# A mixer layer on one core: first column-mean by halves, start-up filler products gathered, and a new written-out order

## The chip, the core and the metric

The kernel runs on one core of a Trainium2 chip. The core has five instruction streams that the text names as the profile does: PE (matrix products), DVE (vector), ACT (activation), POOL (a second vector-like engine) and SP (which here issues the transfers). The metric is device time in microseconds (us); lower is better. All times are of the whole program.

## The reference, cut to what matters

Input is one sequence of 2048 rows of 512. With `xn = layernorm(x)`:

```python
qkv = xn @ wqkv                      # 32 heads of 16
logits = einsum(q, k at 8 positions, 2 apart, looking back) * 16**-0.5   # masked below 0
s = (softmax(logits) @ v) @ wo
y = layernorm(xn)
g = silu(gelu(y @ w1 + b1) @ w2 + b2)        # 512 -> 1376 -> 512
out = x + s * g
```

## The kernel before, in words

The 2048 rows are split by parity into two classes `c` (attention looks back in steps of 2, so each class is closed), and each class into eight tiles of 128 rows, numbered `i` 0 to 7. The heads are split into four blocks `hb`. A unit `u` is one class and one block: `qkv` makes its queries, keys and values on PE, `attention` does the eight-position softmax on DVE with help from POOL and ACT, and the MLP (`mlp1`, `mlp2`) fills PE between. Precise products are made from half-precision high and low parts, so that most products come in three passes: high by high, low by high, high by low.

All work of the opening concerns class 0. The names that matter:

- `xt[i]`, for the tiles 6 and 7 (`FP`): a copy of the tile that arrives already transposed, stored in `U`. `center(i)` subtracts each row's mean: for tile 6 the sum over the four column blocks is taken first (`f`) and one product with a constant matrix, `mean1`, spreads the mean; for tile 7 four products do all of it (L682). The subtraction itself is L693. `direct(i)` then makes the tile's q, k, v in full precision from the raw weights `stq[0]` (L700), tile 6 into `pl`, tile 7 into a bank named `z`.
- The other tiles are normalised row by row: statistics on DVE (L659, L660, L714, L716), a power on POOL (L718), the scaling on POOL, ACT or DVE (L748, L744, L751), the split into high and low parts `yT`, and the transposition: for the tiles 0 to 3 on PE (L766, then the split by L770 to L773), for the tiles 4 to 7 by a transfer of the split parts (L756 to L758).
- `scale_q(hb)`: the sum of squares of a block of weights (L597 on ACT, L513 on PE, L524 to L542 on DVE) gives its scale `qsc`; `prep_q(hb)` makes the high part `wq` on ACT (L619) and the low part (L626 on DVE, L553 and L554 on POOL). `wq_82` and `wq_83` in listings of the order are the blocks 0 and 1.
- `qkv` products are L864; the results leave their bank by L878 on DVE or L882 on ACT.
- Filler products (L1305): `WAKE` products of constants, whose result nobody reads. They are the only PE work that serves no output.

Transfers of the opening are issued by SP one after the other: `t` (the transposed tiles 6 and 7, 256 KB each), `q` (half a block of weights, 384 KB), `x` (a tile, 256 KB), `w` (weights of the MLP).

`Plan` records every operation with what it reads and writes. `Plan.issue` then places the operations in the order of the table `ORDER`, a list of operation numbers; each engine receives its own operations in that order and the waits between engines follow from the reads and writes. So the table alone decides what stands ahead of what on each engine, transfers included, and which buffer of a ring an operation gets.

## Time and profile before

| | us |
|---|---|
| median of three timed runs | 413.33 (413.1 to 413.67) |
| the profiled execution, its own time | 412.45 |
| its span, first to last instruction | 410.6 |
| PE busy | 403.6 |
| DVE busy | 381.7 |
| ACT busy | 225.3 |
| POOL busy | 132.8 |

The profiled execution is 0.9 us below the median of the timed runs. Its span leaves out 1.85 us around it. In a chain row, the columns are start, duration and what ran; in a timeline row start, duration, engine, line, operation and, in brackets, the idle time before it with its releaser. A row `x4` merges four records; a full-precision product leaves two records on PE.

### The profile page before, as it was taken

The page shows a single profiled execution, that of the slowest core. Times are in us where ns is not written, and L with a number is a line of the kernel's source. Part 1 is how long each engine was busy: PE and PEld are TensorE (multiplying, and loading weights), DVE is VectorE, ACT ScalarE, POOL GpSimd, SP SyncE. Part 2 cuts the span into 40 slices and gives each one's busy share as a digit, 9 for nine tenths or more (in the row PEclk, how much of TensorE's full clock was granted, in tenths as well). Part 3 has the DMA queues.
Part 4 walks back from the last instruction along what each step waited for, and adds up shares of the span by engine and source line. Part 5 has one row for each costly group of instructions (what it writes and reads, how often), then busy time and mean ns, then how long its engine had stood idle before and what let it go on. Part 6 is the DMA issues. An engine that isn't in the chain of part 4 may idle for free.

```text
span 410.6 us, 5500 instructions
## 1 busy us (share of the span) xinstructions
PE 403.6 (98%) x2035; PEld 199.3 (49%) x2035; DVE 381.7 (93%) x386; ACT 225.3 (55%) x372; POOL 132.8 (32%) x141
## 2 busy tenths in 40 slices
PE   7999999999999999999999999999999999999996
PEld 4665544444444455445544554444445544444443
DVE  4999999999999999999889999899999989989985
ACT  4899987983989736633564164114523177236310
POOL 3833000053552434243423344233322505250012
PEclk9999999999999999999999999999999999999999
DMA  8947437240018372911251008610244462004874
GB/s 300 388 105 233 165 110 199 89 180 26 1 30 197 77 130 79 165 32 27 51 145 23 0 2 215 208 51 25 104 120 122 107 137 59 0 1 117 271 209 180
DMA packets 52627, 48.04 MB, mean 117 GB/s; under 512 B 37066, under 2 KB 37510, under 8 KB 52088
## 3 DMA queue, kind: packets, MB, share of 16 engines
q1 hardware_dynamic: 52600, 47.69, 41.8%
q8 instruction: 16, 0.26, 0.3%
q14 instruction: 11, 0.09, 0.1%
HBM read 24.40 MB, written 7.34 MB: 77 GB/s over the span
## 4 chain that ended last, share of the span: by engine, by line
PE 97%; DVE 1%; DMA 1%; ACT 0%; issue 0%; ACTq 0%; DVEq 0%
PE ps L864 30%; PE ps L1143 25%; PE z L1186 25%; PE ps L1056 5%; PE z L1088 2%; PE ps L1088 2%; PE z L1174 2%; PE pl L864 1%; PE pl L700 1%; DMA U<-in_A_xt_dram 1%; PE pl L1088 1%; PE z L700 1%; PE z L1177 1%; PE z L766 1%; PE z L1305 0%; DVE U L1120 0%
## 5 line engine op out<-in xcount | busy, mean ns | idle before, releaser
L864 PE MATMUL ps<-wq,yT 128*128 128x384 f16 (+1 forms) x708 | 129.3, 337 | 0.1
L1186 PE MATMUL z<-w,h 128*128 128x512 f16 x480 | 111.4, 379 | 0.0
L1143 PE MATMUL ps<-yT,w 128*128 128x512 f16 x480 | 109.1, 379 | 0.0
L864 PEld LDWEIGHTS <-yT 128*128 128x128 f16 x744 | 72.3, 98 | 58.5 <-issue 1.1
L930 DVE TENSOR_TENSOR prod<-U 128x2048 f32<-128x2048 f32 x32 | 73.8, 2312 | 4.1 <-ACT U L882 3.0
L1143 PEld LDWEIGHTS <-w 128*128 128x128 f16 x480 | 46.7, 98 | 55.6 <-issue 0.5
L933 DVE TENSOR_REDUCE L<-prod 128x128 f32<-128x2048 f32 x32 | 73.0, 2282 | 0.5
L1186 PEld LDWEIGHTS <-h 128*128 128x128 f16 x480 | 46.5, 98 | 54.6 <-issue 0.7
L999 POOL TENSOR_TENSOR prod<-prod,prod 128x1024 f32<-128x1024 f32 x14 | 41.3, 2970 | 81.4 <-DVE prod L988 81.4
L882 ACT ACTIVATE U<-ps,cs 128x384 f32<-128x384 f32 x54 | 30.2, 577 | 62.9 <-PE ps L864 62.7
L988 DVE TENSOR_TENSOR prod<-pl,U 128x2048 f32<-128x2048 f32 x28 | 63.5, 2283 | 0.3
L1156 ACT ACTIVATE ps<-ps,b1T,hsc 128x512 f32<-128x512 f32 x40 | 29.9, 748 | 37.2 <-PE ps L1143 37.0
L1159 ACT ACTIVATE h<-ps,hsc 128x512 f16<-128x512 f32 x40 | 27.4, 685 | 20.5 <-PE z L1186 19.5
L1009 POOL COPY gate<-prod 1x1 f32<-1x1 f32 x21 | 4.6, 221 | 102.2 <-DVE prod L930 102.2
L1010 POOL TENSOR_TENSOR prod<-prod 128x1024 f32<-128x1024 f32 x14 | 32.8, 2346 | 0.0
L1161 DVE SCALAR_TENSOR_TENSOR h<-ps,hsc,h 128x512 f16<-128x512 f32 x40 | 29.5, 744 | 3.3 <-ACT h L1159 3.3
L1056 PE MATMUL ps<-wo,oT 128*128 128x512 f16 x96 | 21.5, 379 | 0.0
L983 DVE TENSOR_TENSOR prod<-prod,prod 128x2048 f32<-128x2048 f32 x9 | 20.6, 2288 | 0.2
L971 ACT ACTIVATE o<-prod,osc 128x1024 f16<-128x1024 f32 (+1 forms) x9 | 9.5, 1052 | 18.1 <-DVE prod L983 9.9
L1010 POOL TENSOR_TENSOR prod<-prod,prod 128x1024 f32<-128x1024 f32 x7 | 16.4, 2347 | 0.0
L1088 PEld LDWEIGHTS <-oT 128*128 128x128 f16 x108 | 10.5, 98 | 10.4 <-issue 0.2
L1056 PEld LDWEIGHTS <-oT 128*128 128x128 f16 x96 | 9.4, 98 | 11.1
(201 smaller groups left out, 397.2 us busy)
## 6 DMA issues: line engine op xcount, KB each, us to landing
f<-in_A_x_dram SPq DMA_DIRECT2D x31, 256.0 KB, 3.1
U<-U SPq DMA_DIRECT2D x16, 392.0 KB, 6.2
gd<-f SPq DMA_DIRECT2D x12, 256.0 KB, 4.3
prod<-in_A_x_dram SPq DMA_DIRECT2D x8, 256.0 KB, 6.2
oT<-in_B_w_dram SPq DMA_DIRECT2D x2, 1024.0 KB
yT<-in_B_w_dram SPq DMA_DIRECT2D x2, 1024.0 KB
f<-gd SPq DMA_DIRECT2D x8, 256.0 KB, 5.0
out_dram<-f SPq DMA_DIRECT2D x8, 256.0 KB
```

The lines of the kernel that those rows point to most:

```text
L864: nc.tensor.matmul(b.t[:, 0:wide], y[:, s, k, o:o + P], wq[hb][:, t, k], start=(n == 0), stop=(n == 11))
L882: act(384, lambda i=i, b=b: nc.scalar.activation(U3[:, i:i + 31:15, :], b.t[:, 0:384].rearrange("p (t e) -> p t e", t=3), AF.Identity, sca ...
L930: dve(2048, lambda p2=p2, g=g: nc.vector.tensor_tensor(p2(), q, slots(Ut, KH, 2 * g), op=ALU.mult), qk + [("kh", ub, 0), ("kh", ub, 1), (" ...
L933: dve(2048, lambda pr=pr, g=g: nc.vector.tensor_reduce(L3()[:, 2 * g:2 * g + 2], pr.t.rearrange("p (r f d) -> p r f d", r=2, d=DH), AX.X, ...
L988: dve(2048, lambda: nc.vector.tensor_tensor(pr.t.rearrange("p (r f d) -> p r f d", r=2, d=DH), A3()[:, 2 * g:2 * g + 2].rearrange("p r (f ...
L999: pool(2.4, lambda n=n: nc.gpsimd.tensor_tensor(acc.t[:, n:n + 1024], acc.t[:, n:n + 1024], p1.t[:, n:n + 1024], op=ALU.add), [acc, p1], [ ...
L1010: nc.gpsimd.tensor_tensor(x.t[:, 0:1024], x.t[:, 0:1024], y(), op=ALU.add)
L1056: nc.tensor.matmul(b.t, oT[:, hb, i // 4, s, i % 4], wo[:, t, hb], start=(hb == 0 and n == 0), stop=(hb == last and n == 2))
L1088: nc.tensor.matmul(b.t[:, cols], oT[:, hb, i // 4, s, i % 4], wo[:, t, hb, cols], start=(start and hb == 0 and n == 0), stop=(stop and hb ...
L1143: nc.tensor.matmul(b.t[0:M], w1[:, s, f * 512 + k * M:f * 512 + (k + 1) * M], yT[ch][:, t, k], start=(n == 0), stop=(n == 11))
L1156: act(512, lambda: nc.scalar.activation(b.t[0:M], b.t[0:M], AF.Gelu_apprx_tanh, bias=b1T[0:M, f:f + 1], scale=hsc[0:M, 1:2]), [b, ("b1T",) ...
L1186: nc.tensor.matmul(z.t, hl[s][:, t * P:(t + 1) * P], w2[:, w, f], start=(f == 0 and n == 0), stop=False)
```

## The change

Three things are edited.

The column sum of tile 6 was one reduction on DVE that reads the 512 columns in a strided view. It becomes two additions that are issued together: the two halves of 256 columns added, then the two 128-column halves of that. The reduction stays in the code, unused.

The number of filler products goes from 24 to 23, and the table places them differently: 19 in a row ahead of the mean product of tile 6 and four right behind it, none later. Before there were seven ahead, three behind, and fourteen singly or in small groups up to 56 us.

The table `ORDER` is another one. It has one number fewer, so that numbers above the filler products are shifted by one; taken with that shift, most operations stand within some twenty places of where they stood, throughout the program, and in the opening the transfers stand in another order. The lines of the kernel after are four higher from `center` on (L864 is L868).

```diff
-MEANBY = ('dve', 'pe', 'pool', 'pool')
+MEANBY = ('halves', 'pe', 'pool', 'pool')
 ...
 ORDER = (
-    0, 1, 240, 19, 2, 3, 4, 5, 6, 7, 8, 9, 10, 11, 133, 129, 113, 120, 112, 115, 130, 20, 21, 32, 33, 168, 114,
+    4, 0, 9, 1, 2, 32, 33, 239, 37, 38, 19, 39, 110, 111, 112, 113, 114, 115, 116, 117, 118, 119, 120, 121, 122,
 ...
-WAKE = 24
+WAKE = 23
 ...
         elif MEANBY[n] == "dve":
             dve(512, lambda: nc.vector.tensor_reduce(f3()[:, 0], x3.rearrange("p k t -> p t k"), AX.X, ALU.add),
                 [("xt", i)], [f], port=False, c=0.45)
+        elif MEANBY[n] == "halves":
+            with pl.fuse():
+                dve(256, lambda: nc.vector.tensor_tensor(f3(), x3[:, 0:2], x3[:, 2:4], op=ALU.add), [("xt", i)], [f])
+                dve(128, lambda: nc.vector.tensor_tensor(f3()[:, 0], f3()[:, 0], f3()[:, 1], op=ALU.add), [f], [f])
```

The transfers of the opening, in the order in which SP issues them (`x0` is tile 0, `q0` and `q2` are the two halves of weight block 0, `q4` and `q6` those of block 1):

| | |
|---|---|
| before | t6, q0, q2, x2, x0, q4, t7, x5, x1, x3, x4, q6, w0, w2, x7, w3, x6, w1, b1 |
| after | x0, t6, x3, q0, q2, x1, t7, x2, q4, x4, x5, w3, q6, x6, x7, w0, w2, w1, b1 |

## Prediction

> **What bounds the kernel now.** I read the page's busy line first:

> ```profile
> PE 403.6 (98%) x2035; PEld 199.3 (49%) x2035; DVE 381.7 (93%) x386; ACT 225.3 (55%) x372; POOL 132.8 (32%) x141
> ```

> Then busy time by stretches of the span (columns: stretch, its length, then busy time and instructions of PE, PEld, DVE, ACT, POOL, the granted clock, the DMA share, GB/s):

> ```profile
> 6.10:30.00 23.90, 23.84 (x132) 14.56 (x133) 20.88 (x60) 19.75 (x39) 13.70 (x12) 1.00 0.80 277
> 60.00:400.00 340.00, 339.91 (x1691) 163.47 (x1690) 323.90 (x271) 175.23 (x285) 110.30 (x114) 1.00 0.38 98
> ```

> From 6.1 to 30 us PE stands idle for 0.06 us, from 60 to 400 us for 0.09. So a gain has three sources only: PE's needed work starts earlier, PE does less that nobody needs, or it does the same faster. From 30 us on the new order can lose and, but for fillers, cannot win. The last additions and stores are the same operations on both sides. That leaves the opening, read in the chain of waits, in order of time (start, duration, what ran):

> ```profile
> 4.54 0.81 PE ps L691 x2
> 5.37 0.70 DVE U L693
> ...
> 6.11 2.93 PE pl L700 x4
> 9.04 0.21 PE z L1305
> ...
> 9.29 0.78 PE pl L700 x2
> 10.06 0.89 PE ps L682 x8
> 10.95 0.65 PE pl L700 x2
> 11.60 0.33 PE z L1305 x3
> ...
> 12.06 0.44 PE z L766 x4
> 12.50 2.58 PE z L700 x8
> 15.10 0.66 PE z L766 x4
> ...
> 17.52 0.64 PE z L766 x4
> 18.16 0.65 PE ps L864 x4
> ...
> 18.95 2.94 PE ps L864 x16
> ...
> 56.17 0.11 PE z L1305
> ```

> Three things are to be seen. The same eight passes over 384 columns take 2.58 us for tile 7 and 2.93 + 0.78 + 0.65 = 4.36 us for tile 6: the first four run at half pace. Then filler products (L1305) stand in the chain: fourteen in eleven rows from 9.04 to 56.17, 1.68 us together. Last, some rows are longer than their work, by waits too short to be named: a transposition (L766) takes 0.44, and twice 0.66 and 0.64; four L864 take 0.65, sixteen should take 2.60 and take 2.94.

> **The half pace.** The granted clock reads 1.00 in every stretch above, so only the durations show it. They change by 9.29 us, after PE had work from 4.54 on. Fillers of the start ran like this (start, duration):

> ```profile
> 1.19 1.65 PE L1305 MATMUL z<-first,fours 128*128 128x256 bf16 x7 [1.19 <-DVE first L440]
> ```

> That is at most 0.24 each, and PE then rested until 4.54. In the kernel after, 19 fillers at 0.21 to 0.24 fill 1.2 to 5.2 or 5.7 us, the mean product and four more follow, so that PE works from 1.2 to nearly 7, longer than the 4.7 us that it took before. I take the passes of tile 6, which now come after 9 us, at full pace.

> [...]

> **When the loads land.** A transfer's landing is seen where an engine started on it with nothing else to wait for:

> ```profile
> 3.46 1.02 DVE L685 TENSOR_REDUCE f<-U 128x128 f32<-128x512 f32 x1 [1.95 <-DMA U<-in_A_xt_dram]
> 4.50 0.84 ACT L597 ACTIVATE wq<-prod 128x768 bf16<-128x768 f32 x1 [2.49 <-DMA prod<-in_A_wqkv_dram]
> 6.35 0.69 DVE L659 BATCH_NORM_STATS2 bn<-prod 128x6 f32<-128x512 f32 x1 [0.29 <-DMA prod<-in_A_x_dram]
> 7.55 0.69 DVE L659 BATCH_NORM_STATS2 bn<-prod 128x6 f32<-128x512 f32 x1 [0.29 <-DMA prod<-in_A_x_dram]
> 8.50 0.84 ACT L597 ACTIVATE wq<-U 128x768 bf16<-128x768 f32 x1 [2.02 <-DMA U<-in_A_wqkv_dram]
> ```

> These are t6, q0, x2, x0 and q4, that is 256, 640, 1280, 1536 and 1920 KB into the stream; the last step is 384 KB in 0.95 us. With the same stream in the new sequence x0 lands at 3.46, t6 (512 KB) near 4.1, q2 (1536) at 7.55, x1 (1792) near 8.2, t7 (2048) at 8.50 + 128 x 0.95 / 384 = 8.82, x2 (2304) near 9.45.

> **The change part by part.** *Halves.* The rows price one addition of 256 columns; that of 128 lies below it.

> ```profile
> 404.56 0.41 DVE L1127 TENSOR_TENSOR U<-U 128x256 f32<-128x256 f32 x1
> ```

> The 128 columns lie between nothing and 0.41; I take 0.3, so 0.7 stands for 1.02 and 0.3 us is saved. It doesn't count: t6 is now the second load, DVE takes tile 0's statistics first, and the mean product moves from 4.54 to about 5.2. On PE nothing needs tile 6 before 9 us.

> *PE's opening.* Before, the first products of tile 6 stand ahead of the sums of weights (L513), and the mean of tile 7 (L682) behind three passes of them:

> ```order
> L700 MATMUL pl_146<-prod_100,U_94 128x384 x2
> L1305 LDWEIGHTS fours
> L1305 MATMUL z_147<-first,fours 128x256
> L513 LDWEIGHTS fours
> L513 MATMUL z_147<-s_126,fours 128x1
> L513 LDWEIGHTS fours
> L513 MATMUL z_147<-s_126,fours 128x1
> L700 MATMUL pl_146<-prod_100,U_94 128x384
> L682 MATMUL ps_144<-U_94,first 128x128 x4
> ```

> After, behind the last filler (L704 is L700 before, L770 is L766):

> ```order
> L1309 MATMUL z_147<-first,fours 128x256
> L513 LDWEIGHTS fours
> L513 MATMUL z_147<-s_125,fours 128x1
> L770 MATMUL z_150<-first,prod_100 128x128 x4
> L513 LDWEIGHTS fours
> L513 MATMUL z_147<-s_125,fours 128x1
> L682 MATMUL ps_144<-U_94,first 128x128 x4
> L704 MATMUL pl_146<-prod_101,U_94 128x384 x2
> L704 MATMUL z_148<-prod_101,U_94 128x384 x2
> ```

> So everything of weight stands behind L682, which waits for t7: PE's unbroken stretch starts at 8.82 instead of 6.11, plus 2.71. Ahead of it only the transposition of tile 0 is done, minus 0.44. The half pace falls into fillers: 4.36 - 2.58, minus 1.78. The fourteen late fillers go: minus 1.68. The short waits in the rows above (0.22 + 0.20 + 0.34) belong to the old order, minus 0.76; new ones take their place.

> *New wait one*: z_148 needs tile 7 centred. On DVE this stands behind the statistics of tile 1, the scale of the weights and the statistics of tile 2:

> ```profile
> 7.08 0.18 DVE L660 BATCH_NORM_AGGREGATE mv<-bn 128x2 f32<-128x6 f32 x1
> 9.36 0.16 DVE L524 TENSOR_SCALAR ssq<-z 128x1 f32<-128x1 f32 x1 [0.71 <-PE z L513]
> 9.87 0.69 DVE L659 BATCH_NORM_STATS2 bn<-prod 128x6 f32<-128x512 f32 x1
> ```

> Statistics take 0.91 (6.35 to 7.08, and 0.18), the scale 0.51 (9.36 to 9.87); its sums need q2, squared from 7.55 on by a pass of 0.84 and its read-out, so they are there near 8.9 and it doesn't wait. From x1 at 8.2 that makes 9.1, 9.6 and 10.5; a small operation of 0.1 and the subtraction of 0.70 follow: 11.3 to 11.4. PE stands there at 8.82 + 0.89 (mean) + 1.29 (two products for pl) = 11.0. Plus 0.4.

> *New wait two*: ACT. Before, both halves of block 1 are made late, between exits of finished banks:

> ```order
> L504 ACTIVATE wq_84,s_129<-h_113 128x4x96
> L756 CAST f_104<-prod_102 128x512
> L619 ACTIVATE wq_83<-U_94,qsc 128x768
> L882 ACTIVATE U_93<-ps_145,cs_118 128x3x128
> L619 ACTIVATE wq_83<-U_94,qsc 128x768
> L882 ACTIVATE U_93<-ps_143,cs_118 128x3x128
> ```

> After:

> ```order
> L504 ACTIVATE wq_84,s_129<-h_113 128x4x96
> L746 ACTIVATE rb_155<-pb_154,rb_155 128x1
> L748 ACTIVATE prod_102<-prod_102,rb_155 128x512
> L760 CAST f_104<-prod_102 128x512
> L619 ACTIVATE wq_83<-U_94,qsc 128x768
> L774 CAST yT_89<-z_147 128x4x128
> L619 ACTIVATE wq_83<-U_94,qsc 128x768
> L774 CAST yT_89<-z_150 128x4x128
> ```

> The exits and one large sum of squares move behind, and PE asks sooner: its first product with block 1 stands behind 12 products of block 0, before behind 36. ACT's work can be priced from start to start:

> ```profile
> 9.99 2.13 ACT L619 ACTIVATE wq<-prod,qsc 128x384 f16<-128x384 f32 x4 [0.56 <-DVE qsc L542]
> 18.18 0.28 ACT L742 ACTIVATE rb<-pb,rb 128x1 f32<-128x1 f32 x1
> 18.50 0.81 ACT L744 ACTIVATE prod<-prod,rb 128x512 f32<-128x512 f32 x1
> 19.22 0.51 ACT L504 ACTIVATE wq<-h 128x384 bf16<-128x384 f32 x1
> 19.73 0.60 ACT L756 CAST f<-prod 128x512 f16<-128x512 f32 x1
> 20.23 0.93 ACT L619 ACTIVATE wq<-U,qsc 128x768 f16<-128x768 f32 x1
> ```

> ACT starts 0.63 us behind L524 (9.36 to 9.99), so at 9.1 + 0.63, about 9.8. From there I leave it no rest: 2.1 (block 0), twice 1.05 (sums of squares of block 1: a pass of 0.84 and its read-out), twice 1.04 (scaling of tiles 1 and 4, 18.18 to 19.22), 0.51, 0.50 (a cast), 0.93, 0.5 (the cast L774), 0.93, together 9.6: it ends at 19.4. PE, from 11.4, has six direct products at 0.65 (3.9), three transpositions (1.32) and twelve L868 (1.95): 18.5. Plus 0.9.

> **The sum.** 2.71 - 0.44 - 1.78 - 1.68 - 0.76 + 0.4 + 0.9 = -0.65, rounded -0.7. Behind this point the products are as many as before, and I count nothing. On the profiled execution's 412.45 this is 411.8; its gap to the median of 413.33 is taken as that execution's, and the forecast is 413.33 - 0.7 = 412.6 us. What is sure of it: pace and fillers are rows. What isn't: t7's landing (8.5 to 9.2), the two new waits (each from nothing to 1.5), the old short waits (0 to 0.76). Without new waits and with t7 early it is -2.2, or 411.1. With both at their upper end and no old wait saved it is +1.8, or 415.1, which needs all three at once.

> **The rivals.** *ACT sets the pace (slower).* Place: the second high half of block 1 (L619). Each us that ACT rests between 9.8 and 19.4 is one on PE. The forecast turns into a loss of 0.8 when that L619 ends at 20.9 instead of 19.4. For: the scaling of tiles 1 and 4 waits for POOL's power, behind DVE's statistics, behind two loads. Against: the wait ahead of L619 in the row above is 0.56 us, none there is of 1.5. Price: 2 us of delay gives 413.33 + 1.3 = 414.6. Chance 0.11.

> *The pace falls back.* Between the last filler, near 6.8, and 8.82 PE has one transposition and two small sums. If this rest lowers the pace again, the mean of tile 7 takes 0.89 more and two products for pl 1.29 more, 2.2; the two new waits swallow 0.4 and 0.9 of it, and 0.9 is left: 413.5. For: before, the rest from 2.84 to 4.54 stood ahead of 4.7 us at half pace. Against: the pace had not risen when that rest came. Chance 0.1.

> [...] No row here shows a pace that falls.

> *The change doesn't do what it says: PE isn't the bound.* DVE is 93% busy, and its chain of attention could hold the end, so that PE's head start is given back in a wait later: 413.3; or PE, under the new table, meets a wait for DVE that the old one avoided, 414.6 if it is 2 us. For: the long stretch without a gap is the old table's merit, and the new one moves operations throughout. Against: DVE rests 16 us of 340 there, PE 0.09. Chance 0.24, 0.1 of it for the wait of 2 us.

> *More than forecast.* The new waits don't come, since ACT and DVE have the loads of x sooner: 411.1 to 412.4. Chance 0.25.

> **How the numbers follow.** The forecast has 0.3, its own range 412.0 to 413.1. About 0.2%, 0.83 us, is what a measurement can tell from no change; faster means under 412.5. Of the forecast half lies there, of "more than forecast" nearly all: 0.15 + 0.25 = 0.4. Slower by over 0.83 (over 414.16): the ACT rival's 0.11, the later wait's 0.1 and 0.03 of the others: 0.24. The rest, 0.36, is within. The range holds 8 of 10: from 411.2, leaving out a tenth at the low end, to 414.6.

> **What would show it.** Right: the first L704 passes at 0.33 each; L682 starting near 8.8 behind a load; no L1309 behind 7 us; PE idle before the first wq_83 product, released by ACT L619, 0.5 to 1 us; none from 30 to 405. Wrong: passes of 0.64 behind 9 us; a PE gap behind 60 us; L682 before 8.2 or behind 9.5; ACT's second L619 of wq_83 ending behind 20.5.

## The result and the profile after

The kernel after takes 414.97 us (median of 20 runs, 412.41 to 417.59) against 413.16 (412.48 to 413.86) for the kernel before: ratio 1.004, interval 1.003 to 1.0051. It is slower by 1.8 us where 0.7 less was forecast, and the median lies above the range of 411.2 to 414.6. The spread is a result by itself: before, it is 1.4 us, after, 5.2.

The profiled execution of the kernel after is one of its short ones: 412.92 us, span 411.1. Its PE stretches, in the columns of the prediction (the second is chosen from the mean of tile 7 to the first twelve products `pl`), and the waits of PE behind 10 us (in total, how often, the longest):

```profile
6.10:30.00 23.90, 21.00 (x118) 12.95 (x118) 20.74 (x58) 20.78 (x39) 11.50 (x11) 1.00 0.81 275
9.69:27.74 18.05, 17.84 (x98) 11.09 (x99) 17.32 (x52) 17.15 (x31) 10.21 (x10) 1.00 0.74 270
60.00:400.00 340.00, 339.45 (x1689) 163.14 (x1688) 323.35 (x270) 176.78 (x289) 110.22 (x109) 1.00 0.38 95
```

```profile
PE ps L868 <- ACT U L886: 0.5, 1, 0.5
PE ps L868 <- ACT wq L619: 0.2, 1, 0.2
```

PE starts its unbroken work later and then is as tight as before, with one new gap of 0.5 us between 60 and 400 us. The chain of waits of the kernel after begins so:

```profile
3.54 6.10 DMA U<-in_A_xt_dram
9.64 0.04 issue
9.69 1.16 PE ps L682 x8
10.85 1.29 PE pl L704 x4
12.14 1.54 PE z L704 x4
...
18.48 0.58 ACT yT L774
19.06 0.84 ACT wq L619
19.90 0.04 issue
19.95 7.96 PE ps L868 x48
```

The load of tile 7 leads, as forecast, but ends at 9.64, not 8.82. From there all is at full pace: four passes take 1.29 or 1.54 us, where the first four took 2.93 before. At 19.95 the wait for ACT's block 1 has come as named, worth 0.21 us. On PE ahead of that (timeline):

```profile
1.19 3.81 PE L1309 MATMUL z<-first,fours 128*128 128x256 bf16 x19 [1.19 <-DVE first L440]
5.16 0.49 PE L695 MATMUL ps<-f,first 128*128 128x128 f32 x2 [0.17 <-DVE pb L720]
5.49 0.60 PE L1309 MATMUL z<-first,fours 128*128 128x256 bf16 x4
7.38 0.16 PE L513 MATMUL z<-s,fours 128*128 128x1 bf16 x1 [1.29 <-ACT wq L597]
7.48 0.63 PE L770 MATMUL z<-first,prod 128*128 128x128 f32 x4
9.34 0.16 PE L513 MATMUL z<-s,fours 128*128 128x1 bf16 x1 [1.23 <-ACT wq L597]
```

Between 6.1 and 9.7 us PE rests, in two waits for ACT's squares, which wait for the loads of q0 and q2. Here nothing came of it. In most other executions something did. The 20 timed runs fall into three groups by the mean granted clock of the run, which leaves out the half pace ahead of the first rise (the profile of before has a mean of 1.000 with its four passes of 2.93 us at 6.11):

| mean granted clock | runs | time, us (median) |
|---|---|---|
| 0.999 to 1.0 | 3 | 412.41 to 412.92 (412.71) |
| 0.995 to 0.996 | 7 | 413.84 to 414.83 (414.17) |
| 0.991 to 0.992 | 10 | 415.1 to 417.59 (415.4) |

In the kernel before every run of the later comparisons has 0.998 to 1.0. Half a clock through 3.41 us, the step between the changes in e0's profile, lowers the mean over a span of some 412 by 0.5 x 3.41 / 412 = 0.0041, so the groups fit none, one and two stretches of 3.41 us at half pace; the profile of e0, with one, has a mean of 0.995, that of h1, with two, 0.992. A mean of 0.998 is no such stretch: at the very end of the program, where PE has no work left, the clock falls once more (in the profile of after it is 1.00 from 407.2 to 410.6 us and 0.54 from there to 411.1; the last product ends at 407.18). In e6's profile, with a mean of 0.998, the 0.002 make 1.6 us at half, worked out from its span of 411.7. The next section shows the stretches.

### The profile page after: what moved, and what is told of

The parts are those of the page before. It is cut to its first block, busy times and chain, and to the rows that moved or that the text cites. A ratio compares the mean times of both kernels' runs of the same rounds, so it can differ in the third digit from the quotient of the medians.

```text
span 411.1 us, 5501 instructions
## 1 busy us (share of the span) xinstructions
PE 402.3 (98%) x2034; PEld 199.0 (48%) x2034; DVE 381.5 (93%) x387; ACT 225.8 (55%) x373; POOL 132.4 (32%) x141
## 4 chain that ended last, share of the span: by engine, by line
PE 92%; DVE 3%; DMA 1%; issue 1%; ACT 1%; SPq 1%; DVEq 0%
PE ps L868 27%; PE ps L1147 25%; PE z L1190 24%; PE ps L1060 5%; PE z L1092 2%; PE ps L1092 2%; PE z L1178 2%; DMA U<-in_A_xt_dram 1%; PE pl L868 1%; PE z L704 1%; PE pl L704 1%; PE pl L1092 1%; PE z L1181 1%; DVE lw L643 1%; DVE L L937 1%
## 5 line engine op out<-in xcount | busy, mean ns | idle before, releaser
L868 PE MATMUL ps<-wq,yT 128*128 128x384 f16 (+1 forms) x708 | 128.1, 337 | 0.8 <-ACT U L886 0.5
L868 PEld LDWEIGHTS <-yT 128*128 128x128 f16 x744 | 72.5, 98 | 59.2 <-issue 2.3
L886 ACT ACTIVATE U<-ps,cs 128x384 f32<-128x384 f32 x54 | 30.5, 578 | 78.5 <-PE ps L868 61.9
L1003 POOL TENSOR_TENSOR prod<-prod,prod 128x1024 f32<-128x1024 f32 x14 | 37.3, 2683 | 98.6 <-DVE prod L992 71.7
L1014 POOL TENSOR_TENSOR prod<-prod,prod 128x1024 f32<-128x1024 f32 x7 | 16.4, 2346 | 0.0
L1092 PEld LDWEIGHTS <-oT 128*128 128x128 f16 x108 | 10.5, 98 | 10.4 <-DMA oT<-o 0.2
```

The lines of the kernel that those rows point to most:

```text
L868: nc.tensor.matmul(b.t[:, 0:wide], y[:, s, k, o:o + P], wq[hb][:, t, k], start=(n == 0), stop=(n == 11))
L886: act(384, lambda i=i, b=b: nc.scalar.activation(U3[:, i:i + 31:15, :], b.t[:, 0:384].rearrange("p (t e) -> p t e", t=3), AF.Identity, sca ...
L1003: pool(2.4, lambda n=n: nc.gpsimd.tensor_tensor(acc.t[:, n:n + 1024], acc.t[:, n:n + 1024], p1.t[:, n:n + 1024], op=ALU.add), [acc, p1], [ ...
L1014: nc.gpsimd.tensor_tensor(x.t[:, 0:1024], x.t[:, 0:1024], y(), op=ALU.add)
L1092: nc.tensor.matmul(b.t[:, cols], oT[:, hb, i // 4, s, i % 4], wo[:, t, hb, cols], start=(start and hb == 0 and n == 0), stop=(stop and hb ...
```

## The experiments

Two theories stood beside each other. **P**: the pace falls back in PE's rest. **L**: the loads of the opening land later and at times that change from run to run.

**e0: the kernel after, once more.**

> The kernel after, once more, as the control of this group. Theory P (the pace falls back: PE rests from about 6.1 to 9.7 us but for 0.9 us of work, and in most executions this takes the array to half pace for one or two stretches of 3.4 us): times in clusters near 412.5, 414.2 and 415.4 us, with mean granted clocks of 1.000, 0.996 and 0.992, and a profile of one of the slower ones shows passes of 0.64 us somewhere between 7 and 17 us. Theory L (the spread comes from loads that land at different times): times spread without clusters, and the clock does not follow them.

414.61 us (412.99 to 416.02), ratio 1.0035 (1.002 to 1.005); clocks 0.992 to 0.996 in all 12 runs. So the falls are there, but the times don't cluster as P expected: the nine runs with one stretch lie between 412.99 and 415.39, the three with two between 414.84 and 416.02. Something else spreads them too. The profile shows a fall. PE by stretches of 3.41 us, cut at the changes of the granted clock (stretch, length, busy and count, granted clock, DMA share, GB/s), and the rows on PE there:

```profile
5.40:8.81 3.41, 1.62 (x11) 1.00 1.04 396
8.81:12.22 3.41, 3.06 (x11) 0.50 1.04 397
12.22:15.63 3.41, 3.41 (x12) 1.00 1.07 421
```

```profile
7.92 0.16 PE L513 MATMUL z<-s,fours 128*128 128x1 bf16 x1 [1.63 <-ACT wq L597]
...
9.32 2.08 PE L682 MATMUL ps<-U,first 128*128 128x128 f32 x8 [0.19 <-DMA U<-in_A_xt_dram]
11.19 1.97 PE L704 MATMUL pl<-prod,U 128*128 128x384 f32 x4
```

The pace rose at 5.40 (nineteen fillers from 1.19 take 4.21 us, the four from 5.69 take 0.60); in the stretch that followed PE was busy for 1.62 of 3.41 us; the next one ran at half: the mean of tile 7 took 2.08 us for 1.16. Tile 7 landed earlier than in the first profile (9.32 against 9.69), and still the span is 411.9 us, 0.8 longer.

**e1: the rest filled.** Thirty more fillers, 12 ahead of the first L513, 14 ahead of the second, 4 ahead of L682.

> The kernel after with 30 more filler products in PE's rest, 12 ahead of the first weight sum, 14 ahead of the second, 4 ahead of the mean of tile 7; nothing else moves. Theory P: every execution keeps full pace, clock 1.000 (0.999), times 412.3 to 413.2 with the spread of the kernel before, median 2 us below the kernel after. Theory L: the spread of 412.4 to 417.6 stays and the median is 415.

414.45 us (412.96 to 415.06), ratio 1.0025 (1.0013 to 1.0038). All clocks are 0.998 to 1.0: no falls. But the median is over 1 us above the range that P gave, since L682 starts at 10.89 behind fillers, 1.2 us later than in the profile of after: overfilled, it could not tell the price.

**e6 and e9: the right dose.** The edit of e6's table; e9 has the first six alone:

```diff
-  ..., 132, 34, 50, 35, 26, ...
+  ..., 132, [six fillers], 34, 50, [five fillers], 35, 26, ...
```

Operation 34 is the first L513, 35 the second.

> The kernel after with eleven more fillers, six ahead of the first product of squares (L513) and five ahead of the second: PE is busy for part of its rest between 6 and 9.7 us, and L682 isn't pushed back as in e1. Theory P (the pace falls after the rest, in some executions): the granted clock stays at 0.998 or more in all timed runs, and the median comes to 413.0 to 413.6, 1.0 to 1.6 under the kernel after. Theory L (the loads of x and of the squares land later, and at other times from run to run): clock up or not, the time stays at 414.0 to 414.8 with a spread of 2 us or more. By both together: 413.5 to 414.2, with the low end near 412.5.

> The kernel after with six more fillers instead of e6's eleven, all ahead of the first L513: half the dose. By theory P falls become rarer, not all gone: granted clocks of 0.991 to 0.996 in a part of the runs, and a median between e6's 413.4 and the 414.6 to 415 of after: 413.6 to 414.4. If six are enough: clocks all at 0.998 or more, 413.2 to 413.6.

e6: 413.38 us (412.24 to 414.73), ratio 1.001 (0.9997 to 1.0023), clocks 0.998 to 1.0 in all 12. e9: 413.23 (412.11 to 414.99), ratio 1.0004 (0.9991 to 1.0018), one run of 12 with 0.996, the longest. So theory P holds: work that nobody reads, put into the rest, takes 1.2 to 1.6 us off the kernel after, and six fillers do as much as eleven. Theory L is wrong on the time, but right on the spread: with no fall at all e6's runs still lie 2.5 us apart, those of before beside them 1.4. The profile of e9, in the two stretches behind its rise, has more work than e0's had:

```profile
4.82:8.23 3.41, 2.76 (x20) 1.00 1.02 337
8.23:11.65 3.42, 2.36 (x13) 1.00 1.05 401
```

**e2: no fillers at all.**

> The kernel after without any of its 23 fillers. Theory P: PE works too little before 9.7 us to raise its pace, so no early rise and no fall: the clock rises once, after 9.7 us plus one to two windows of 3.4 us, at 13 to 16.5 us, and the same mean work at half pace costs every run what two falls cost: clocks (counted from the first rise) at 0.998 or more and 415 to 416, with less spread than after. If the early rise does nothing for the time: 414.0 to 414.6.

414.71 us (six runs, 414.29 to 415.35), ratio 1.004 (1.0027 to 1.0053), clocks 0.998 to 1.0. L682 starts at 9.46 and takes 2.08 us; the pace rises at 13.07 and stays (four passes take 2.33 us from 11.32, four 1.45 from 13.49). The time lies between the two expectations. So the 23 fillers, as the change places them, bring the median nothing: 414.97 and 414.61 with them, 414.71 without. They trade one late rise for an early rise and one or two falls.

**h1 and h2: the order cut in two.** h1 has the first 400 operations of the new order and the rest in the old one; h2 the reverse (with 23 fillers: the last of before's late ones, near 56 us, is missing).

> The new opening alone: the first 400 operations in the new order (with halves and fillers as after), and the rest in the order of before. If the whole loss is in the opening: 414.2 to 414.8, and the later gap of 0.5 us near 110 us (PE waiting for ACT's U, L886) is gone without changing that. If the later order costs 0.5 us: 413.8 to 414.3. Theory P: granted clocks of 0.991 to 0.996 in most runs, as after.

> The reverse: the first 400 operations, the fillers and the mean as before, and the rest in the new order. If the loss is in the opening: 413.0 to 413.4, clocks 0.998 or more. If the later order costs 0.5 us by a wait for ACT near 110 us: 413.6 to 414.0 with PE's gap there in the profile. An order that is cut in two can leave a wait of its own at the seam near 30 us, which the profile would show.

h1: 414.5 us (412.22 to 419.42), ratio 1.0028 (1.0013 to 1.0043; it leaves out the run of 419.42 us), 10 of 11 runs with clocks of 0.988 to 0.996, where 0.988 would, by the sum above, be three stretches. Its profile caught two half stretches in a row:

```profile
4.97:8.39 3.42, 1.21 (x9) 1.00 0.95 351
8.39:11.80 3.41, 3.10 (x15) 0.50 1.05 404
11.80:15.22 3.42, 3.42 (x7) 0.50 1.07 413
```

How long PE rests hangs on the load of q0. ACT starts on it so in after, e0 and h1, which share their opening (no half stretch behind the rise, one, and two):

```profile
6.39 0.84 ACT L597 ACTIVATE wq<-prod 128x768 bf16<-128x768 f32 x1 [4.38 <-DMA prod<-in_A_wqkv_dram]
```

```profile
6.93 0.84 ACT L597 ACTIVATE wq<-prod 128x768 bf16<-128x768 f32 x1 [4.92 <-DMA prod<-in_A_wqkv_dram]
```

```profile
7.54 0.84 ACT L597 ACTIVATE wq<-prod 128x768 bf16<-128x768 f32 x1 [5.53 <-DMA prod<-in_A_wqkv_dram]
```

PE rests ahead of its first L513 for 1.29, 1.63 and 2.24 us in the three. So the two theories meet: the later the load, the longer the rest and the deeper the fall. These are three executions and no test of it.

h2: 413.68 us (412.74 to 413.92), ratio 1.0009 (1.0 to 1.0018), clocks 0.998 to 1.0. The opening carries most of the loss. The order behind it costs 0.5 us by h2, at the edge of what can be told from noise; h1 doesn't show it, since its gap near 110 us is gone and its median is only 0.1 to 0.5 under the kernel after, in the range given for a loss that is all in the opening. The next two runs decide. In h2 there was no wait at the seam near 30 us; the wait was the one near 110 us (0.47) that the kernel after has too:

```profile
110.97 5.02 PE L868 MATMUL ps<-wq,yT 128*128 128x480 f16 x24 [0.51 <-ACT U L886]
```

```profile
109.07 1.15 ACT L565 ACTIVATE wo<-yT,osc 128x1024 f16<-128x1024 f32 x1 [3.77 <-DVE osc L537]
110.12 0.32 ACT L890 ACTIVATE hl<-ps,hsc 128x96 f32<-128x96 f32 x1
110.35 0.57 ACT L886 ACTIVATE U<-ps,cs 128x384 f32<-128x384 f32 x1
```

(Both are of the kernel after, PE and ACT.) ACT stands for 3.77 us in front of the scaling of `wo`, for whose scale DVE isn't ready; behind it, in ACT's queue, is the exit that frees PE's next bank. In the kernel before the exit stands ahead of the same scaling:

```profile
108.81 0.57 ACT L882 ACTIVATE U<-ps,cs 128x384 f32<-128x384 f32 x1
109.28 1.14 ACT L565 ACTIVATE wo<-yT,osc 128x1024 f16<-128x1024 f32 x1
```

**e8: both costs taken away.** h1 with e6's eleven fillers.

> The new opening (first 400 operations) with e6's eleven more fillers in PE's rest, and the rest in the order of before: both suspected costs are taken away at once. If the loss of the kernel after is the pace that falls back (some 1.2 us: h1 against e6 and h2) and the wait for ACT near 110 us in the new order (0.5 us: h2), and nothing else, the two add up: 412.7 to 413.2, clocks 0.998 or more, no gap near 110 us. If the loads of x that land later cost something by themselves: 413.4 or more, with a spread of over 2 us.

412.83 us (411.94 to 413.65), ratio 0.9994 (0.9986 to 1.0003), clocks 0.999 to 1.0 but for two runs of 0.998. Against h1, whose opening it shares but for the fillers, it is 1.7 us less: a second price for the falls. The two costs add up, and no loss against before is left.

**e10: one operation moved.** e6, with operation 305 (the scaling of `wo`) behind the four exits that waited in its queue; every other engine's instructions are unchanged.

```diff
-  ..., 288, 305, 466, 468, 467, 475, 469, 471, 470, 481, 307, ...
+  ..., 288, 466, 468, 467, 475, 469, 471, 470, 305, 481, 307, ...
```

> e6 with one ACT operation moved: the scaling of wo (L565), which waits 3.8 us for DVE's osc with finished banks' exits (L886, L890) queued behind it, is put behind the four exits. If this one wait is what the order behind the 400th operation costs (e6 against e8 0.55 us, h2 against before 0.5): 412.8 to 413.0, no gap of PE near 110 us, DVE and all else as in e6. If the gap only moves (to the next exits, or to DVE waiting for the scaled wo): 413.2 to 413.6 with another gap behind 100 us.

412.71 us (411.85 to 414.79), ratio 0.998 (0.9968 to 0.9991): 0.67 below e6, though measured on another chip, where before took 413.31 and not 413.19. The gap is gone, not moved:

```profile
105.63 12.31 PE L868 MATMUL ps<-wq,yT 128*128 128x480 f16 x60
```

So the 0.5 us is this one wait: one operation moved, and the interval lies clear of e6's. The profiled run (414.79 us) is the one of 12 in which the pace fell: its first L513 stands at 9.39 us behind the load of q0, against 7.38 in the profile of after, and for such a rest (1.89 us ahead of that L513) eleven fillers were too few:

```profile
6.57:9.98 3.41, 1.52 (x14) 1.00 1.01 374
9.98:13.40 3.42, 3.42 (x17) 0.50 1.04 387
```

**e3, e4, e5, e7: the kernel before with single edits.** e3 has eight more fillers ahead of the mean of tile 6, e4 the sum by halves, e5 no late fillers (`WAKE` from 24 to 10), e7 all three.

> The kernel before with 8 more filler products ahead of the mean product of tile 6, so that PE has work from 1.2 to 4.4 us and beyond without a rest. Theory P: the array is at full pace before or soon after 6.1 us, the four passes of tile 6 take 1.3 us instead of 2.9, and the time falls by 0.8 to 1.6 us against the kernel before (411.6 to 412.4). Theory L has nothing to say on the clock; under it the opening waits for loads, and the gain is below 0.4 us.

> The kernel before with the sum by halves alone. The mean product of tile 6 comes 0.3 us sooner. Theory P: PE's needed work starts 0.3 us sooner while the pace rises at the same time, so 0 to 0.3 us faster (412.9 to 413.2). Theory L: the same, since the tile itself has landed; a change of over 0.5 us either way would speak against both.

> The kernel before without its fourteen late fillers (those between the transpositions and the products for pl). The prediction put them at 1.68 us on the path. If so: 411.5 to 412.2, ratio 0.996 to 0.9975. If they stand in waits of PE for loads and for DVE that last anyway: 413.0 to 413.4, ratio within 0.999 to 1.0005. If without them the pace falls back in some executions: slower, 414, with granted clocks under 0.997.

> The kernel before with the three edits that helped it or did no harm: eight fillers ahead of the first mean (e3, -0.35), its first mean by halves (e4, -0.2), its fourteen late fillers gone (e5, -0.6); its order else unchanged. If they add up: 412.0 to 412.2. If they all buy the same wait for the load of tile 7: 412.5 to 412.7, as e5 alone. If the pace falls back without the late fillers, now that it rises early: clocks under 0.997 and 413.5 or more.

e3: 412.87 us, ratio 0.9989 (0.9979 to 0.9999). The pace is up early and tile 6's first four passes take 1.56 us, 1.4 less than in the profile of before. The gain is 0.35, short of what P expected, since PE then waits for the same load:

```profile
5.98 1.56 PE L700 MATMUL pl<-prod,U 128*128 128x384 f32 x4 [0.45 <-DVE U L693]
...
9.45 1.16 PE L682 MATMUL ps<-U,first 128*128 128x128 f32 x8 [1.02 <-DMA U<-in_A_xt_dram]
```

e4: 412.99 us, ratio 0.9993 (0.9982 to 1.0003): no difference that can be told. e5: 412.58, ratio 0.9983 (0.9974 to 0.9992): 0.61 us, between the two expectations. PE now shows two waits that fillers had covered (lines of e5 are one lower than those of before):

```profile
15.52 0.66 PE L765 MATMUL z<-first,prod 128*128 128x128 f32 x4 [0.34 <-ACT prod L743]
...
17.93 0.66 PE L765 MATMUL z<-first,prod 128*128 128x128 f32 x4 [0.43 <-DVE prod L750]
```

e7: 412.24 us (411.98 to 412.71), ratio 0.9979 (0.997 to 0.9988): 0.95 below before, against 1.2 for the three summed, with the smallest spread of all. It has the lowest median of the kernels tried.

## Why the prediction was wrong, by its steps

**The step that failed is "I take the passes of tile 6, which now come after 9 us, at full pace".** Of the kernel after's 32 timed runs, 29 lose one or two stretches to half pace behind the rise (clocks of 0.991 to 0.996). The rival "The pace falls back" named the place, the rest between the last filler and the load of tile 7, and had a chance of 0.1. Its price of 0.9 us was also short: the groups of the first table lie 1.5 and 2.7 us above the one without a fall. Part of that may be the load, since a later q0 goes with a longer rest (6.39, 6.93 and 7.54 us above); filling the rest brought 1.2 to 1.6 us (e6) and 1.7 (e8 against h1). The rival set 1.3 us against its price for the waits that a fall would swallow; these waits measured 0.21. The mistake was to give nothing for a fall in the sum because the half pace of before came ahead of the rise, when no row of before could show what a rest does behind it.

No long gap was needed: the longest in e0 behind the rise is 1.63 us, and the pace fell.

**The sum, where the pace holds**, can be read from L682 to the first twelve products `pl` (L868), in profiles with and without a fall:

| kernel | L682 starts | first `pl` of twelve | between | half pace behind L682's start | span |
|---|---|---|---|---|---|
| e8 | 8.94 | 26.98 | 18.04 | none | 410.3 |
| e9 | 9.45 | 27.50 | 18.05 | none | 411.0 |
| after | 9.69 | 27.74 | 18.05 | none | 411.1 |
| e6 | 9.97 | 28.04 | 18.07 | none | 411.7 |
| e0 | 9.32 | 28.52 | 19.20 | 2.9 us | 411.9 |
| h1 | 9.89 | 30.29 | 20.40 | 5.3 us | 413.5 |

Without a fall the stretch is 18.04 to 18.07 us in these four (17.71 in e1, where L682 comes at 10.89), so a later start of L682 goes almost whole into the kernel. That start varies from 8.94 to 9.97 us between executions. It is the landing of tile 7 where PE waits for that load (9.32 to 9.89 in after, e0, e2, e9 and h1); in e6 and e8 PE goes from L513 to L682 without a wait for a load. In before, the same products stand between 6.11 and 27.47 us, 21.36. The change is -3.31, where the terms between came to -0.44 - 1.78 - 1.68 - 0.76 + 0.4 + 0.9 = -3.36, or -3.03 without the three fillers that stand behind 27.47 (0.33).

- **"L682 starts when t7 lands, 8.82"**: mis-sized. Measured 9.69, so the term is +3.58, not +2.71. The stream was assumed to run as before; in the first 11 us it moved 3.13 MB, before 3.38, which is one tile of 256 KB less. The other profiles agree: 265 to 296 GB/s in these 11 us in the nine with the new opening, 295 to 309 in the six with the old. Tile 7 is the seventh transfer in both sequences, and it didn't land sooner for the 128 KB less ahead of it: with the old sequence PE waits for it until 9.45 in e3. Why the new sequence moves less wasn't tried. The rows of the transfers, first of before, then of after:

```profile
DMA packets 1612, 3.38 MB, mean 307 GB/s; under 512 B 174, under 2 KB 174, under 8 KB 1612
```

```profile
DMA packets 1493, 3.13 MB, mean 284 GB/s; under 512 B 159, under 2 KB 160, under 8 KB 1493
```

- **The two new waits, +1.3**: too much. PE shows none for tile 7's subtraction, which DVE ends at 12.06 and PE, itself later than forecast, takes up at 12.12; and 0.21 for ACT, whose second L619 ends at 19.90 (forecast 19.4).
- **Half pace, -1.78**: the sixteen passes take 6.94 us before, and by the chain 1.29 + 1.54 + 0.75 + 0.65 + 0.75 + 0.65 = 5.63 after; -1.31. As a gain of the whole it was mis-founded: e3 gave before that pace, and all but 0.35 us went into the wait for tile 7.
- **Late fillers, -1.68**: alone worth 0.61 (e5). Part of them stood in waits.
- That the terms between come within 0.3 us of the measured change is luck: waits forecast too long stand against savings forecast too large.

The opening so comes out at +0.27, in an execution without a fall, where the terms give -0.32 up to there (-0.65 without the 0.33). Both profiles are of short executions, before's 0.7 us under the median of its 20 runs and after's 2.0, so this isn't the change of the medians.

**"Behind this point I count nothing"** missed 0.5 us (in the two profiles the part behind the first `pl` is 0.2 longer, the wait of 0.5 less the 0.33 of fillers). The rival of a later wait had 0.1, with a price of 2 us; e10 shows the wait and its cause. The place was in the order for ACT: a wait for DVE with bank exits behind it, which is what the prediction had looked for in the opening only.

**What was right**: the load of tile 7 heads the chain; no filler stands behind 7 us; the wait for ACT's block 1 is there; the halves bring nothing that can be told (e4). Of the marks set for being wrong, L682 behind 9.5, a gap of PE behind 60 us and, in e0 and h1, slow passes behind 9 us all came.

**The whole**: an opening that gains 0.4 to 0.6 us in the medians where the pace holds and the later wait is gone (e8, e10, both with the rest partly filled), plus 0.5 to 0.7 for that wait (h2, e6 against e8 and e10), plus 1.2 to 1.6 for falls (e0 and after against e6). That makes 1.1 to 1.9; measured were 1.4 (e0) and 1.8.

## What to carry to other kernels

Filler products raised the pace early here (at 5.40 us in e0, without any at 13.07 in e2), but they had to go on until the real work arrived: 23 of them followed by 3 us of mostly rest gave as much as none, and six more in the rest gave the loss back. Look at the granted clock of every timed run, not of one profile: the profile taken first was one of three runs in 20 that showed nothing. The scaling that waited for DVE held what stood behind it in ACT's queue (3.77 us on ACT, 0.5 us on PE), so exits of banks go ahead of such an operation. The best kernel of all is before with three small edits (e7, -0.95): the old order was worth keeping.

## What was not expected of the hardware

```profile
4.45:7.86 3.41, 1.95 (x16) 1.00 0.95 305
```

The whole length of a rest doesn't decide it: e0 fell with one of 1.63 us, while e6 held with one of 1.65, which spans the end of one stretch and the start of the next, at 7.37:

```profile
8.66 0.16 PE L513 MATMUL z<-s,fours 128*128 128x1 bf16 x1 [1.65 <-ACT wq L597]
```

Whether it is the work in a stretch or the longest rest inside it, these rows can't tell: that rest is 1.6 us and more where the pace fell, 1.3 and less where it held.

Coming back is harder to tell: e0 rose after a half stretch with 3.06 us busy, h1 didn't after one with 3.10. Before the first rise the stretches show a granted clock of 1.00 although passes run at half pace (before: 1.00 from 5.79 to 9.20, with the four passes of 2.93 us in it), so here that column, and the mean made from it, tell something only from the first rise on.
